# A planned order of work with new transfer and engine times, and a convolution whose taps are summed by TensorE for two blocks

## The chip, the cores and the metric

The kernel runs on one core of a Trainium2 chip. The metric is the device time of one execution in microseconds (us); lower is better. TensorE does the matrix products, VectorE (DVE) and ScalarE (ACT) the elementwise work, SyncE (SP) issues nearly all transfers.

## The reference

A softmax-weighted causal convolution over 7 tokens, then two MLPs with 2048 hidden units, on 8192 tokens of 192 features:

```python
def _attn_ref(x, weight_gen):                    # x (2, 4096, 192), weight_gen (2, 4096, 8, 7)
    w = softmax of weight_gen over its last axis
    x_unf = the 7 tokens up to each token, zeros in front
    out = np.einsum('bshk,bskhg->bshg', w, x_unf)
def _moe_ref(x, w_in, w_out):
    h = np.maximum(x @ w_in, 0.0)
    return h * h @ w_out
def _moe2_ref(x, w_in, w_out):
    h = x @ w_in
    return (h * np.clip(h + 3.0, 0.0, 6.0) / 6.0) @ w_out
```

The weights of the MLPs come as 64-bit floats; everything else is 32-bit. Matrix products are made in a rounded 32-bit format from a high and a low part of each operand, three products for one.

## The kernel before

**Tiling.** Each of 128 partitions holds 64 tokens in a row. They are taken in 16 blocks of 4 tokens per partition (512 columns, N). A block goes through the convolution, the first MLP (m=0) and the second (m=1). A *step* (m, b, f) is one block against 2 of the 16 tiles of the hidden units, so there are 2 x 16 x 8 = 256 steps. Step i issues part A (18 half-height products into the PSUM tile `h`) and, three steps later (LAG), part B (20 half-height products into the accumulators `accN` and `accR`), woven together in `emit_pair` (L299 is where each product is issued; the three last steps have only B, at L357). Between A and B the elementwise work stands: `relu` (L382, ACT), `square` (L386, ACT) or `gate` (L395, DVE), `high` (L402, either), `low` (L408, DVE).

**The convolution** of a block (`convolve`) is 7 products on DVE (L614) and 6 additions on DVE (L628). Then, for every block but block 0, `turn` (L276, DVE) and `to_dram` (L285, four transfers) turn the result through a DRAM tile `xs`, `from_dram` (L268, two transfers) brings it back with features on partitions, and `split_hi` (L224) and `split_lo` (L230) make its two parts. Block 0 is turned on TensorE instead: `twice` (L242), `turn_pe` (L250), `split_pe_hi` (L256), `split_pe_lo` (L261). The softmax of a chunk is seven small instructions (L575 to L595), the exponential on ACT (L583). `load_first` issues ten transfers for block 0; `load_rest` brings the other half of chunk 0.

**The weights** of one group (2 hidden tiles) come by four transfers (`load_weights`, L89 and L95) into a tile `st` with two buffers, and are made into high and low parts by six instructions on DVE (L117, L130, L139, L154, L161 twice) and four on ACT (L124, L127, L148, L151). There are 8 groups for each MLP; step f of a block needs group f/2.

**The order.** All instructions are written out by a planner in the kernel's own code. Every piece of work is an `Op` with a guessed duration per engine, what it depends on, and which buffers it takes. A loop simulates four engines (PE, ACT, DVE, SP), starts on each the ready piece with the earliest due time, and so fixes the order in which each engine's queue is filled. On the chip each queue is in order: an instruction that waits holds all behind it. A guessed duration therefore changes no work, only the order. A transfer has one guessed time for its issue (0.15 to 0.7 us for a whole group) and a fixed time to landing.

**The order of steps.** Blocks 0 and 1 of the first MLP are woven from step 4 (WEAVE): a0 a1 a2 a3, then a4 c0 a5 c1 and so on, so block 1 is needed at step 5 and block 2 at step 16. Six blocks of the first MLP (LEAD) run before the first of the second, which is woven with the next block; then blocks of the two alternate; six blocks of the second MLP are left at the end.

Of the kernel before, what the change touches and what calls it, by code (L numbers as in the profile page):

```python
# [8 lines left out]
F32 = mybir.dt.float32  # L9
# [9 lines left out]
def conv_moe_moe2_kernel(  # L19
# [10 lines left out]
    nc = tc.nc  # L30
# [18 lines left out]
    LEAD = 6  # L49
# [18 lines left out]
    ps_a = ctx.enter_context(tc.tile_pool(name="ps_a", bufs=4, space=bass.MemoryType.PSUM))  # L68
# [122 lines left out]
    def load_first():  # L191
        chunk_tiles(0)
        xt = xc[0]
        nc.sync.dma_start(out=wc[0][:, 0:TB, :], in_=w_v[:, 0:TB, :])
        nc.sync.dma_start(out=xt[:, PAD:PAD + TB, :], in_=x_v[:, 0:TB, :])
        for b in range(B):
            nc.gpsimd.memset(xt[b * PB:b * PB + 1, 0:PAD, :], 0.0)

        for h0, h1 in ((PAD // 2, PAD), (0, PAD // 2)):
            for b in range(B):  # L200
                p0 = b * PB
                for r0, r1 in ((0, (PB - 1) // 16 * 16), ((PB - 1) // 16 * 16, PB - 1)):
                    nc.sync.dma_start(
                        out=xt[p0 + 1 + r0:p0 + 1 + r1, h0:h1, :],
                        in_=x_v[p0 + r0:p0 + r1, TPP - PAD + h0:TPP - PAD + h1, :],
                    )
# [30 lines left out]
    def twice(j, engine):  # L237
        if j == 0:
            xraw[0, 0] = x_tile()
        d = xraw[0, 0][:, j].rearrange("p (t h r) -> p t h r", t=TB, h=2)  # L240
        src = attn[0][:, :, j * HP:(j + 1) * HP].unsqueeze(2).to_broadcast([P, TB, 2, HP])
        copy_on(engine)(d, src)  # L242

    def turn_pe(j):
        if j % 2 == 0:
            xps[j] = ps_h.tile([P, 2, N], F32, tag="h", name="xt")
        d = xraw[0, 0][:, j].rearrange("p (t c) -> p t c", t=TB)
        pv = xps[j // 2 * 2][:, j % 2].rearrange("d (q t r) -> d t q r", q=Q, t=TB)
        for t in range(TB):
            nc.tensor.transpose(pv[:, t], d[:, t], ident)  # L250

    def split_pe_hi(j, engine):
        if j == 0:
            xs_in[0, 0] = [split_tile(n) for n in "hl"]
        n = min(2, NK - j)
        copy_on(engine)(xs_in[0, 0][0][:, j:j + n], xps[j][:, 0:n])  # L256

    def split_pe_lo(j):
        n = min(2, NK - j)
        hi, lo = [v[:, j:j + n] for v in xs_in[0, 0]]  # L260
        nc.vector.tensor_tensor(out=lo, in0=xps[j][:, 0:n], in1=hi.bitcast(F32), op=ALU.subtract)  # L261
# [240 lines left out]

    class Op:
        def __init__(self, fn, times, deps, takes, uses, lands):
            self.fn, self.times, self.takes, self.lands = fn, times, takes, lands
# [5 lines left out]
    WEAVE = 4  # L511
# [4 lines left out]
    HOP, SLOT, T0 = 0.1, 0.2158, 20.0  # L516
    ops, users, taken = [], {}, {k: [] for k in BUFS}

    def add(times, fn, deps=(), takes=(), uses=(), lands=0.0):
        o = Op(fn, times, list(deps), list(takes), list(uses), lands)  # L520
        ops.append(o)
        for key in o.takes + list(uses):
            if o not in users.setdefault(key, []):
                users[key].append(o)
        return o

    def two(cols):
        return 0.165 + 1.03e-3 * cols

    def act_t(cols):  # L530
        return 0.19 + 0.83e-3 * cols

    def cp(cols):
        return {"ACT": act_t(cols), "DVE": 0.165 + 0.52e-3 * cols}
# [6 lines left out]
    first_load = add({"SP": 0.7}, load_first, takes=[("xc", 0), ("wc", 0)], lands=3.0)  # L541
    rest_load = None
    for m in range(2):
        for g in range(NG):
            k = (m, g)
            deps = [(last, -99.0)] if last else [(first_load, -99.0)]
            ld = last = add({"SP": 0.3}, lambda k=k: load_weights(*k), deps, [("st", k)], lands=4.0)
            if rest_load is None:
                last = rest_load = add(
                    {"SP": 0.15}, load_rest, [(ld, -99.0)], uses=[("xc", 0), ("wc", 0)], lands=3.0  # L550
                )
            q = add({"DVE": 0.61}, lambda k=k: w_q(*k), [ld], [("q", k)], [("st", k)])
            r = add({"ACT": 0.84}, lambda k=k: w_relu(*k), [q], uses=[("q", k)])
            t0 = add({"ACT": 1.14}, lambda k=k: w_t0(*k), [ld], [("t", k)], [("st", k)])
            t1 = add({"DVE": 0.68}, lambda k=k: w_t1(*k), [ld], [("t", k)], [("st", k)])
            hb = add({"DVE": 1.08}, lambda k=k: w_hb(*k), [r], [("hb", k)], [("st", k), ("q", k)])
            hi_w[k] = add(cp(CAN), lambda e, k=k: w_hi(*k, e), [hb], uses=[("hb", k)])
            hi_r[k] = add(cp(CR), lambda e, k=k: r_hi(*k, e), [hb], uses=[("hb", k)])
            sc = add({"DVE": 0.56}, lambda k=k: w_sc(*k), [hb], uses=[("q", k), ("hb", k)])
            both = [sc, t0, t1]  # L560
            lo_w[k] = add({"DVE": 0.82}, lambda k=k: w_low(*k), both, uses=[("q", k), ("t", k)])
            lo_r[k] = add({"DVE": 0.29}, lambda k=k: r_low(*k), both, uses=[("q", k), ("t", k)])

    chunk_load = {0: first_load}
    soft = {}

    def softmax(c, t0, t1, load):
# [31 lines left out]
        o = add({"DVE": two(cols)}, s1, [load], [st], keys)  # L599
# [37 lines left out]

    conv = {}
    for b in range(NB):
        c, t0 = divmod(b * TB, CT)  # L640
        if b == 0:
            s = softmax(0, 0, TB, first_load)
        elif b == 1:
            s = softmax(0, TB, CT, rest_load)
        elif t0 == 0:
            chunk_load[c] = add(
                {"SP": 0.15}, lambda c=c: load_chunk(c), [(conv[b - 1], -99.0)], [("xc", c), ("wc", c)], lands=6.5
            )
            s = softmax(c, 0, CT, chunk_load[c])
        conv[b] = convolve(b, [s] + ([(conv[b - 1], -99.0)] if b else []))  # L650
# [30 lines left out]
    def x_chain(m, b, source):  # L681
# [4 lines left out]
        o = prev = add({"SP": 0.15}, lambda: from_dram(m, b), deps, [key], uses, lands=6.0 if m else 5.0)  # L686
# [4 lines left out]

    dups = [
        add(cp(N), lambda e, j=j: twice(j, e), [conv[0]], [("x", (0, 0))], [("a", 0)]) for j in range(NK)
    ]
    for j in range(1, NK):
        dups[j].deps.append((dups[0], -99.0))
    turns_pe = []
    for j in range(NK):
        key = ("h", ("xt", j // 2 * 2))
        deps = [dups[j]] + turns_pe[-1:]  # L700
        turns_pe.append(add({"PE": 0.9}, lambda j=j: turn_pe(j), deps, [key], [("x", (0, 0))]))
    splits = [("sh", (0, 0)), ("sl", (0, 0))]
    hi_pe, lo_pe = [], []
    for j in range(0, NK, 2):
        key, cols = ("h", ("xt", j)), min(2, NK - j) * N
        t = {"ACT": act_t(cols), "DVE": two(cols)}
        deps = [turns_pe[min(j + 1, NK - 1)]] + hi_pe[-1:]
        hi_pe.append(add(t, lambda e, j=j: split_pe_hi(j, e), deps, splits if j == 0 else [], [key] + splits))
        lo_pe.append(add({"DVE": two(cols)}, lambda j=j: split_pe_lo(j), hi_pe[-1:], uses=[key] + splits))
    x_ready = {(0, 0): lo_pe}  # L710
    prev = hi_pe[0]

    ready_g, step_ops = {}, []
    stored, fixed = {}, {}

    def prepare_x(m, b):
        if m == 0:
            t = add({"DVE": two(TB * D)}, lambda: turn(b), [conv[b]], [("pr", ("aT", b))], [("a", b)])
            w = add({"SP": 0.3}, lambda: to_dram(b), [t], [("xs", b)], [("pr", ("aT", b))], lands=2.0)
# [8 lines left out]
    def finish(m, b, step):  # L728
# [6 lines left out]
        if m == 0:  # L735
            stored[b] = add({"SP": 0.15}, lambda: store_y(b), [z[0], z[1]], [("ys", b)], zk, lands=2.7)
            due(stored[b], fixed[step] + 30)
            return
        s0 = add({"SP": 0.1}, lambda: store_z0(b), [z[0]], [("zs", b)], zk[:1], lands=2.0)
        f0 = add({"ACT": act_t(N)}, lambda: fold(b), [z[1], (s0, -99.0)], [("zq", ("u", b))], zk[1:])  # L740
        f1 = add({"DVE": two(N)}, lambda: fold_add(b), [f0], uses=[("zq", ("u", b))] + zk[1:])
        s1 = add({"SP": 0.1}, lambda: store_z1(b), [f1], uses=[("zs", b)] + zk[1:], lands=2.3)
        l1 = add({"SP": 0.3}, lambda: load_z(b), [s0, s1], [("zq", b)], [("zs", b)], lands=2.3)
        tz = add({"DVE": two(TB * D)}, lambda: turn_z(b), [l1], [("q", ("o", b))], [("zq", b)])
        so = add({"SP": 0.1}, lambda: store_out(b), [tz], uses=[("q", ("o", b))], lands=2.5)
        due(so, fixed[step] + 45)

    prev_pe = turns_pe[-1]
    for i in range(NS + LAG):
        A = steps[i] if i < NS else None  # L750
        Bs = steps[i - LAG] if i >= LAG else None
        deps, takes, uses = [(prev_pe, -HOP)], [], []
# [55 lines left out]
    def released(o):  # L808
        t = 0.0
        for d, lag in o.deps:  # L810
            same = len(o.times) == 1 and len(d.times) == 1 and o.times.keys() == d.times.keys()
            t = max(t, d.start + 1e-6, d.end + lag + (0.0 if same else HOP))
# [7 lines left out]
    def available(o, t):  # L820
        wait = t
        for cls, key in o.takes:
# [3 lines left out]
            if len(held) >= BUFS[cls]:  # L826
                for u in users[cls, held[-BUFS[cls]]]:
                    if u.end is None:
                        return float("inf")
                    wait = max(wait, u.end + HOP)  # L830
        return wait

    t = 0.0
    while len(order) < len(ops):
        later = float("inf")
        for e in ("PE", "ACT", "DVE", "SP"):
# [18 lines left out]
            best.end = free[e] + best.lands  # L855
            later = min(later, free[e])
# [53 lines left out]
```

## Time and profile before

| | |
|---|---|
| median of three runs | 1142.57 us (1141.55 to 1144.91) |
| the profiled execution | 1142.03 us, span 1140.2 us |
| first product of step 0 | 36.27 us after the span's start |
| last product | ends near 1134.3 us |

The span runs from the first to the last instruction; 1.83 us of the profiled execution lie outside it. PE is TensorE's products, PEld its weight loads, SPq the issue of transfers. TensorE was recorded at its high clock level for most of the span, and at a lower mean between 36 and 76 us.

### The profile page before, as it was taken

How to read it: one execution, taken by the hardware profiler on the slowest of the kernel's cores; microseconds unless marked ns; L12 is line 12 of the kernel's file. 1: busy time of each engine (PE TensorE's matmuls, PEld its weight loads, DVE VectorE, ACT ScalarE, POOL GpSimd, SP SyncE). 2: the span in 40 equal slices, each digit the busy share in tenths (PEclk: the TensorE clock that was granted, in tenths of full speed). 3: DMA queues.
4: the chain of work that ended last, by engine and by line, in shares of the span. 5: the costliest groups of instructions: out<-in, count | busy, mean ns of one | idle time of the engine just before them, and what ended most of it. 6: DMA issues, size and time to landing. Idle time of an engine off the chain costs nothing.

```text
span 1140.2 us, 23704 instructions
## 1 busy us (share of the span) xinstructions
PE 1072.3 (94%) x9722; PEld 930.5 (82%) x9722; DVE 937.5 (82%) x1011; ACT 601.9 (53%) x657; POOL 4.3 (0%) x11
## 2 busy tenths in 40 slices
PE   0579999999999999999999999999999999999998
PEld 0368878887888888788888888888888888888887
DVE  6969989899899898889888887675867768888886
ACT  2669888897565647656364544435253442233322
POOL 0000000000000000000000000000000000000000
PEclk9979999999999999999999999999999999999999
DMA  5442424542241423314132221202222221232101
GB/s 139 119 118 71 146 74 143 128 107 66 71 108 36 138 70 115 82 43 123 33 84 57 75 66 52 70 21 69 57 71 56 51 66 39 60 79 74 34 25 47
DMA packets 68756, 87.90 MB, mean 77 GB/s; under 512 B 5612, under 2 KB 44396, under 8 KB 67752
## 3 DMA queue, kind: packets, MB, share of 16 engines
q1 hardware_dynamic: 68504, 86.19, 27.9%
q8 instruction: 76, 1.25, 0.5%
q14 instruction: 32, 0.26, 0.1%
q10 hardware_dynamic: 144, 0.20, 0.0%
HBM read 59.89 MB, written 26.48 MB: 76 GB/s over the span
## 4 chain that ended last, share of the span: by engine, by line
PE 72%; DVE 12%; DMA 9%; ACT 2%; issue 2%; SPq 2%; DVEq 0%; ACTq 0%
PE h L299 34%; PE accN L299 22%; PE accR L299 15%; DMA x<-ys 4%; DVE gl L408 3%; DMA st<-in_moe_w_out_dram 2%; DVE pr L614 2%; DVE a L628 2%; DVE sl L230 1%; DVE g L395 1%; ACT g L382 1%; DMA x<-xs 1%; DMA xs<-aT 1%; ACT gh L402 1%; DMA zs<-z 1%
## 5 line engine op out<-in xcount | busy, mean ns | idle before, releaser
L299 PE MATMUL h<-sh,w 64*128 64x512 f32 x3072 | 618.9, 382 | 27.8 <-ACT w L148 15.3
L299 PE MATMUL accN<-gh,w 64*128 64x512 f32 x2024 | 519.9, 377 | 0.0
L382 ACT ACTIVATE g<-h 128x1024 f32<-128x1024 f32 x256 | 261.9, 1023 | 465.3 <-PE h L299 442.2
L299 PEld LDWEIGHTS h<-sh,w 64*128 64x128 f32 x3072 | 387.9, 189 | 78.3 <-ACT w L148 17.6
L299 PE MATMUL h<-sl,w 64*128 64x512 f32 x1536 | 442.7, 380 | 1.3 <-DVE sl L230 1.3
L299 PEld LDWEIGHTS accN<-gh,w 64*128 64x128 f32 x2024 | 378.3, 187 | 26.6
L408 DVE TENSOR_TENSOR gl<-g,gh 128x1024 fp32r<-128x1024 f32 x256 | 312.6, 1221 | 30.0 <-ACT gh L402 20.1
L299 PE MATMUL accR<-gl,r 64*128 64x512 f32 x1012 | 301.4, 378 | 3.7 <-DVE gl L408 3.5
L299 PE MATMUL accN<-gl,w 64*128 64x512 f32 x1012 | 301.4, 378 | 0.0
L299 PE MATMUL accR<-gh,r 64*128 64x512 f32 x1012 | 300.6, 377 | 0.0
L299 PEld LDWEIGHTS h<-sl,w 64*128 64x128 f32 x1536 | 240.6, 189 | 21.8 <-DVE sl L230 1.6
L299 PEld LDWEIGHTS accR<-gl,r 64*128 64x128 f32 x1012 | 188.6, 187 | 19.4 <-DVE gl L408 6.3
L299 PEld LDWEIGHTS accR<-gh,r 64*128 64x128 f32 x1012 | 189.1, 187 | 13.4
L299 PEld LDWEIGHTS accN<-gl,w 64*128 64x128 f32 x1012 | 188.6, 187 | 13.2
L402 DVE CAST gh<-g 128x1024 fp32r<-128x1024 f32 x136 | 94.1, 692 | 89.3 <-PE accN L299 87.8
L395 DVE SCALAR_TENSOR_TENSOR g<-g,h 128x1024 f32<-128x1024 f32 x128 | 155.5, 1215 | 8.4 <-ACT g L382 7.8
L402 ACT CAST gh<-g 128x1024 fp32r<-128x1024 f32 x120 | 125.1, 1042 | 22.5 <-PE accN L299 19.3
L386 ACT ACTIVATE g<-g 128x1024 f32<-128x1024 f32 x128 | 135.5, 1059 | 1.9
L628 DVE TENSOR_TENSOR a<-a,pr 128x768 f32<-128x768 f32 x96 | 91.6, 954 | 0.4
L614 DVE TENSOR_TENSOR pr<-xc,wc 128x768 f32<-128x768 f32 x96 | 90.8, 953 | 1.2 <-DMA xs<-aT 0.8
L230 DVE TENSOR_TENSOR sl<-x,sh 128x1536 fp32r<-128x1536 f32 x31 | 54.3, 1753 | 12.8 <-ACT sh L224 12.8
L250 PE MATMUL xt<-ident,x 128*128 128x128 f32 x12 | 2.8, 424 | 30.6 <-ACT x L242 30.6
(60 smaller groups left out, 328.0 us busy)
## 6 DMA issues: line engine op xcount, KB each, us to landing
x<-ys SPq DMA_DIRECT2D x32, 512.0 KB, 6.4
x<-xs SPq DMA_DIRECT2D x30, 384.0 KB, 4.9
xc<-in_x_dram SPq DMA_DIRECT2D x7, 1344.0 KB, 5.9
ys<-z SPq DMA_DIRECT2D x32, 256.0 KB, 2.3
st<-in_moe_w_in_dram SPq DMA_DIRECT2D x32, 192.0 KB, 3.6
xs<-aT SPq DMA_DIRECT2D x60, 96.0 KB, 3.4
zq<-zs SPq DMA_DIRECT2D x60, 96.0 KB, 2.3
out_dram<-o SPq DMA_DIRECT2D x15, 384.0 KB, 2.3
```

What stands on the lines that cost most here:

```text
L230: nc.vector.tensor_tensor(out=lo, in0=src, in1=hi.bitcast(F32), op=ALU.subtract)
L250: nc.tensor.transpose(pv[:, t], d[:, t], ident)
L299: return lambda: nc.tensor.matmul(ps, w[r], turns(x[r]), start=start, stop=stop)
L382: nc.scalar.activation(g, ps, AF.Relu, bias=3.0 if m else 0.0)
L386: nc.scalar.activation(g, g, AF.Square)
L395: nc.vector.scalar_tensor_tensor(out=g, in0=g, scalar=6.0, in1=h_ps[m, b, f], op0=ALU.min, op1=ALU.mult)
L402: copy_on(engine)(gh, g)
L408: nc.vector.tensor_tensor(out=gl, in0=g, in1=gh.bitcast(F32), op=ALU.subtract)
L614: nc.vector.tensor_tensor(out=dst, in0=xs, in1=ws.to_broadcast([P, TB, H, G]), op=ALU.mult)
L628: nc.vector.tensor_tensor(out=total(), in0=total(), in1=prods.pop((b, k)), op=ALU.add)
```

## The change

1. Blocks 0 and 1 (ON_PE = 2): the 7 products stay on DVE, each in a tile of its own; their sum is made by TensorE with two 32-bit products per tap against the identity (384 columns each) in an accumulator tile. Both blocks are turned on TensorE; block 1 leaves the path through DRAM. `twice` now reads PSUM, in two halves.
2. `load_first` is split into three pieces, so that the softmax of block 0 depends on the weights' transfer alone, and each tap on the transfer that it reads. The softmax of the second half of chunk 0 may be placed only after the last sum of block 0 has been placed.
3. The planner's guesses: every transfer has an issue time and a service time on one shared line, plus FLIGHT 1.6; a waiting compute piece counts it as LATE 1.0 later; PSUM or buffers read by TensorE come free SLACK 0.5 later; instruction times are lowered by some 0.1 us.
4. WEAVE 4 to 3: block 1 is needed at step 4. LEAD 6 to 8: eight blocks of the first MLP in front, eight of the second at the end.
5. The two accumulators of a block become one tile of two PSUM banks (2 buffers in place of 4).

```diff
-    LEAD = 6
+    LEAD = 8
-    def twice(j, engine):
+    def twice(b, j, engine):
...
+        src = attn[b][:, :, 0:2 * D].rearrange("p a (t d) -> p a t d", t=2)[:, :, :, j * HP:(j + 1) * HP]
+        for a in range(2):
+            copy_on(engine)(d[:, 2 * a:2 * a + 2], src[:, a].unsqueeze(2).to_broadcast([P, 2, 2, HP]))
...
+    FLIGHT = 1.6
+    LATE = 1.0
+    SLACK = 0.5
+    WEAVE = 3
+    ON_PE = 2
...
-            ld = last = add({"SP": 0.3}, lambda k=k: load_weights(*k), deps, [("st", k)], lands=4.0)
+            ld = last = add(
+                None, lambda k=k: load_weights(*k), deps, [("st", k)],
+                dmas=[(0.62, 1.1), (0.62, 0.9), (0.6, 0.72), (0.47, 0.38)],
+            )
...
+    def convolve_pe(b, deps):
...
+        def total(k):
+            if k == K - 1:
+                attn[b] = ps_a.tile([P, 2, N], F32, tag="acc", name="acc")
+            v = prods.pop((b, k)).rearrange("p t h g -> p (t h g)")
+            for a in range(2):
+                nc.tensor.matmul(
+                    attn[b][:, a, 0:2 * D], ident, v[:, a * 2 * D:(a + 1) * 2 * D], start=k == K - 1, stop=k == 0
+                )
...
+            t = add(
+                {"PE": 1.4}, lambda k=k: total(k), [o] + ([t] if t else []), [acc] if k == K - 1 else [], [key, acc]
+            )
...
-            s = softmax(0, 0, TB, first_load)
+            s = softmax(0, 0, TB, [w_first])
         elif b == 1:
-            s = softmax(0, TB, CT, rest_load)
+            s = softmax(0, TB, CT, [rest_load, (conv[0], -99.0)])
...
-        o = prev = add({"SP": 0.15}, lambda: from_dram(m, b), deps, [key], uses, lands=6.0 if m else 5.0)
+        o = prev = add(
+            None, lambda: from_dram(m, b), deps, [key], uses, dmas=[(0.6, 2.7 if m else 2.0), (0.6, 2.4 if m else 1.7)]
+        )
...
+            late = LATE if d.dmas and lag > -9 and not o.dmas else 0.0
+            t = max(t, d.start + 1e-6, d.end + lag + late + (0.02 if same else HOP))
```

## Rows read from the trace of the kernel before

**Rows 1.** The page, first part: busy us, share of the span, instructions.
```profile
span 1140.2 us, 23704 instructions
...
PE 1072.3 (94%) x9722; PEld 930.5 (82%) x9722; DVE 937.5 (82%) x1011; ACT 601.9 (53%) x657; POOL 4.3 (0%) x11
```

**Rows 2.** Busy time by stretch: stretch, length, each engine's busy us, granted clock, DMA.
```profile
36.20:80.00 43.80, 28.22 (x156) 21.14 (x158) 33.06 (x48) 24.51 (x31) 0.00 (x0) 0.81 0.58 154
...
124.50:200.00 75.50, 73.17 (x672) 63.80 (x674) 69.08 (x76) 63.34 (x72) 0.00 (x0) 1.00 0.41 120
200.00:280.00 80.00, 76.49 (x700) 65.50 (x698) 71.23 (x84) 67.52 (x79) 0.00 (x0) 1.00 0.42 103
...
500.00:960.00 460.00, 459.49 (x4252) 402.65 (x4250) 353.77 (x363) 208.22 (x217) 0.00 (x0) 1.00 0.24 63
...
1134.30:1140.20 5.90, 1.38 (x12) 1.22 (x12) 0.56 (x1) 1.07 (x2) 0.00 (x0) 0.76 0.19 67
```

**Rows 3.** Chain that ended last, in order of time: start, us, what.
```profile
81.63 1.08 PE h L299 x10
...
85.73 1.08 PE h L299 x10
```

**Rows 4.** Busy time by stretch, products of L299 alone (PE, PEld, clock, DMA).
```profile
36.20:124.50 88.30, 71.34 (x550) 58.02 (x550) 0.90 0.43 114
```

**Rows 5.** Timeline of the first 37 us: start, us, engine, line; idle before and releaser.
```profile
2.91 0.39 DVE L575 TENSOR_REDUCE st<-wc 128x32 f32<-128x224 f32 x1 [2.91 <-DMA wc<-in_weight_gen_dram]
...
3.76 0.39 ACT L583 ACTIVATE wc<-wc 128x224 f32<-128x224 f32 x1 [1.52 <-DVE wc L578]
...
11.33 1.05 ACT L127 COPY t<-st 128x768 uint16<-128x768 uint16 x1 [7.18 <-DMA st<-in_moe_w_out_dram]
11.76 0.39 DVE L575 TENSOR_REDUCE st<-wc 128x32 f32<-128x224 f32 x1 [8.04 <-DMA wc<-in_weight_gen_dram]
...
12.49 0.38 DVE L586 TENSOR_REDUCE st<-wc 128x32 f32<-128x224 f32 x1
...
13.94 0.96 DVE L614 TENSOR_TENSOR a<-xc,wc 128x768 f32<-128x768 f32 x1
14.81 0.95 DVE L614 TENSOR_TENSOR pr<-xc,wc 128x768 f32<-128x768 f32 x1
...
27.84 1.95 DVE L628 TENSOR_TENSOR a<-a,pr 128x768 f32<-128x768 f32 x2
...
30.59 2.79 PE L250 MATMUL xt<-ident,x 128*128 128x128 f32 x12 [30.59 <-ACT x L242]
...
36.27 0.80 PE L299 MATMUL h<-sh,w 64*128 64x512 f32 x2 [2.89 <-DVE sl L261]
```

**Rows 6.** Groups by line and shape of the first 122 us: busy, mean ns.
```profile
L130 DVE TENSOR_SCALAR t<-st 128x768 uint16<-128x768 uint16 x9 | 5.9, 658 | 0.0
```

**Rows 7.** Busy time by stretch, instructions that touch tile q alone (DVE, ACT).
```profile
0.00:124.50 124.50, 26.55 (x41) 6.70 (x8) 0.93 0.42 113
```

**Rows 8.** One line's instructions: count, ns min/median/max, first and last start.
```profile
L494 PE MATMUL ot<-x x8: 222/275/294, 1135.1 to 1136.1; 128*128 128x64 f32 x8
```

**Rows 9.** Timeline of 49 to 71 us.
```profile
49.28 0.98 DVE L276 STREAM_TRANSPOSE aT<-a 128x768 f32<-128x768 f32 x1
...
56.83 0.80 PE L299 MATMUL h<-sh,w 64*128 64x512 f32 x2 [5.06 <-ACT w L148]
...
65.28 1.47 ACT L224 CAST sh<-x 128x1536 fp32r<-128x1536 f32 x1 [7.36 <-DMA x<-xs]
...
70.62 0.79 PE L299 MATMUL h<-sh,w 64*128 64x512 f32 x2 [6.81 <-ACT w L148]
```

**Rows 10.** Busy time of PE in one stretch (busy, products, granted clock, DMA).
```profile
70.60:75.80 5.20, 5.18 (x24) 0.50 0.57 151
```

**Rows 11.** Timeline of two later places where PE waits.
```profile
148.91 1.47 ACT L224 CAST sh<-x 128x1536 fp32r<-128x1536 f32 x1 [4.46 <-DMA x<-xs]
...
151.36 0.48 PE L299 MATMUL h<-sh,w 64*128 64x512 f32 x2 [2.15 <-ACT g L382]
...
258.64 0.67 DVE L117 TENSOR_SCALAR q<-st 128x768 uint32<-128x768 uint32 x1 [3.68 <-DMA st<-in_moe_w_out_dram]
...
264.55 0.48 PE L299 MATMUL accR<-gl,r 64*128 64x512 f32 x1 [2.26 <-DVE gl L408]
```

More of the change, by code (lines that the diff above doesn't have):

```diff
@@ L316, in make_B @@
         if f == 0:
-            accs[m, b] = [ps_a.tile([P, N], F32, tag="acc", name=f"acc{n}") for n in "NR"]
+            acc = ps_a.tile([P, 2, N], F32, tag="acc", name="acc")
+            accs[m, b] = [acc[:, o] for o in range(2)]
         high, low = [[], []], [[], []]
@@ L540, in conv_moe_moe2_kernel @@
     last = None
-    first_load = add({"SP": 0.7}, load_first, takes=[("xc", 0), ("wc", 0)], lands=3.0)
+    both = [("xc", 0), ("wc", 0)]
+    w_first = add(None, load_w0, takes=both, dmas=[(0.42, 0.3)])
+    x_first = add(None, load_x0, [(w_first, -99.0)], uses=both[:1], dmas=[(0.43, 1.66)])
+    halos = []
+    for h in ((PAD // 2, PAD), (0, PAD // 2)):
+        dep = halos[-1] if halos else x_first
+        halos.append(add(None, lambda h=h: load_halo(*h), [(dep, -99.0)], uses=both[:1], dmas=[(0.42, 0.25)] * 4))
+    first_load = halos[-1]
     rest_load = None
@@ L551, in conv_moe_moe2_kernel @@
                 )
[L552 to L556, printed above, removed]
+            q = add({"DVE": 0.55}, lambda k=k: w_q(*k), [ld], [("q", k)], [("st", k)])
@@ L597, in s7 @@
             )
-        o = add({"DVE": two(cols)}, s1, [load], [st], keys)
+        o = add({"DVE": two(cols)}, s1, load, [st], keys)
         o = add({"DVE": two(cols)}, s2, [o], uses=[st] + keys)
@@ L636, in convolve, with needs, term @@
         return add(cost, lambda: summed(0), [o], uses=[("a", b), ("pr", (b, 0))])
+    def needs(b, k):
+        if b:
+            return []
+        return [x_first] if k == PAD else [halos[k < PAD // 2]]
+    def convolve_pe(b, deps):
+        c, t0 = divmod(b * TB, CT)
+        keys, acc = [("xc", c), ("wc", c)], ("acc", ("conv", b))
+        def term(k):
+            xs = xc[c][:, t0 + k:t0 + k + TB, :].rearrange("p t (h g) -> p t h g", h=H)
+            ws = wc[c].rearrange("p t (h k) -> p t h k", k=K)[:, t0:t0 + TB, :, k:k + 1]
+            prods[b, k] = att.tile([P, TB, H, G], F32, tag="pr", name="pr", bufs=2)
+            nc.vector.tensor_tensor(out=prods[b, k], in0=xs, in1=ws.to_broadcast([P, TB, H, G]), op=ALU.mult)
+        def total(k):
[6 more added lines that the diff above has]
+                )
+        o = t = None
+        for k in range(K - 1, -1, -1):
+            key = ("pr", (b, k))
+            more = ([o] if o else deps) + needs(b, k)
+            o = add({"DVE": two(TB * D)}, lambda k=k: term(k), more, [key], keys)
+            t = add(
+                {"PE": 1.4}, lambda k=k: total(k), [o] + ([t] if t else []), [acc] if k == K - 1 else [], [key, acc]
+            )
+        return t
     conv = {}
@@ L702, in conv_moe_moe2_kernel @@
[L702 to L710, printed above, removed]
@@ L711, in conv_moe_moe2_kernel, with x_on_pe @@
-    prev = hi_pe[0]
+    x_ready, x_turned = {}, {}
+    def x_on_pe(b):
+        nonlocal prev
+        deps = [conv[b]] + ([(prev, -99.0)] if prev else [])
+        acc = ("acc", ("conv", b))
+        dups = []
+        for j in range(NK):
+            t = {"ACT": 2 * act_t(N // 2), "DVE": 2 * (0.09 + 1.045e-3 * N // 2)}
+            dups.append(
+                add(t, lambda e, j=j: twice(b, j, e), deps + [(d, -99.0) for d in dups[:1]], [("x", (0, b))], [acc])
+            )
+        turns_pe, hi_pe, lo_pe = [], [], []
+        for j in range(NK):
+            key = ("h", ("xt", b, j // 2 * 2))
+            t = {"PE": 1.0}
+            turns_pe.append(add(t, lambda j=j: turn_pe(b, j), [dups[j]] + turns_pe[-1:], [key], [("x", (0, b))]))
+        splits = [("sh", (0, b)), ("sl", (0, b))]
+        for j in range(0, NK, 2):
+            key, cols = ("h", ("xt", b, j)), min(2, NK - j) * N
+            t = {"ACT": act_t(cols), "DVE": two(cols)}
+            deps = [turns_pe[min(j + 1, NK - 1)]] + hi_pe[-1:]
+            takes = splits if j == 0 else []
+            hi_pe.append(add(t, lambda e, j=j: split_pe_hi(b, j, e), deps, takes, [key] + splits))
+            t = {"DVE": two(cols)}
+            lo_pe.append(add(t, lambda j=j: split_pe_lo(b, j), hi_pe[-1:], uses=[key] + splits))
+        x_ready[0, b] = lo_pe
+        prev = hi_pe[0]
+        return turns_pe[-1]
@@ L713, in conv_moe_moe2_kernel @@
+    first_turn = x_on_pe(0)
     ready_g, step_ops = {}, []
@@ L829, in available @@
                         return float("inf")
-                    wait = max(wait, u.end + HOP)
+                    wait = max(wait, u.end + (SLACK if "PE" in u.times else HOP))
         return wait
-    t = 0.0
+    t = line_free = 0.0
     while len(order) < len(ops):
@@ L855, in conv_moe_moe2_kernel @@
             best.end = free[e] + best.lands
+            if best.dmas:
+                at = t
+                for issue, serve in best.dmas:
+                    at += issue
+                    line_free = max(line_free, at + FLIGHT) + serve
+                best.end = line_free
             later = min(later, free[e])
```

126 lines of the change are left out of this document (63 added, 63 removed).

## The prediction

> **What bounds the kernel now.** I read the page first: TensorE is busy for 94% of the span, DVE for 82% [rows 1], so TensorE's own work is the floor and the question is where it falls behind. The chain that ended last gives its rate: a full step of 38 half products takes 4.10 us [rows 3], 0.1079 us for each. The code issues 256 steps x 38 = 9728 of them, 1049.6 us. The span is 1140.2 us, so some 90 us are something else, and the table by stretch says where. I cut the span at four points: step 0 begins at 36.27 us [rows 5]; up to 124.5 us 550 half products ran [rows 4], which is about the 548 that stand before step 16 (16 x 18 + 13 x 20), where block 2 is first needed; the last product ends near 1134.3 us, and 5.9 us follow [rows 2].
>
> - Before step 0: 36.2 us.
> - Step 0 to 16: 88.3 us for 59.3 us of work (550 x 0.1079), so **29.0 us lost** [rows 3, 4].
> - After that: 1009.8 us for 9178 x 0.1079 = 990.3 us, so **19.5 us lost**.
> - End: 5.9 us. Sum 1140.2.
>
> The three losses have causes that the timeline names. **Before step 0**, DVE reduces the first weights at 2.91 us and is then idle for 8.04 us until 11.76, since the reduction for the second half of the chunk was placed ahead of the second reduction of the first half and its transfer had not landed; the exponential that block 0 needed ended at 4.15 us (3.76 + 0.39) [rows 5]. **Step 0 to 16**: block 1 was turned on DVE at 49.28 us, but ACT's copy of it started at 65.28, after 7.36 us of idling for the transfer from `xs`. Weight work stood behind it in ACT's queue, and TensorE waited 5.06 and 6.81 us for ACT's weights [rows 9]. After such a wait TensorE runs at its low level, 1.2 GHz: in 5.20 us it did 24 products at a granted clock of 0.50 [rows 10]; at 0.1079 us they are 2.6 us. **After step 16** the places are small and of one kind: ACT idles 4.46 us for block 3's transfer and TensorE then 2.15 us; DVE idles 3.68 us for weights and TensorE then waits 2.26 us [rows 11]. From 500 to 960 us PE is busy 459.49 of 460.00 us [rows 2]; nothing is to be had there.
>
> **The change part by part.**
>
> *Step 0 comes earlier.* The second half's softmax can no longer stand ahead of block 0's. After the exponential's end at 4.15, the second reduction may start near 4.2; in the trace 1.45 us lie from it (12.49) to the first tap product (13.94), so the first product starts near 5.65. Seven products at 0.87 us (13.94 to 14.81) are 6.1 us [rows 5]. One group of weights must be ready too: five of its six DVE instructions write or read tile q, 26.55 us for 8 groups, 3.3 us each, and L130 adds 0.66 [rows 6, 7], so 4.0 us. They can start when the weights land, 11.33 [rows 5], and I don't expect the added splits of the loads to move that. DVE's last product ends near 5.65 + 6.1 + 4.0 = 15.8, the last sum on TensorE near 17.2. From the last addition's end (27.84 + 1.95 = 29.8) to step 0 (36.27) there were 6.5 us of copying, turning and splitting [rows 5], which stay. Step 0 then starts at about 24, **12 us earlier**. Bounds: 20 if the weights come wholly between the products, 31 if TensorE's sums are slow (next).
>
> *TensorE gets new work.* Block 0's sums fall before step 0, where PE had nothing to do, and cost nothing as long as a tap isn't slower than DVE's 0.87 us plus what lies between. Block 1's sums and turns fall among steps 0 to 4, on the path. No row shows a 32-bit product of 384 columns. From below: a rounded 64x512 product costs 0.2158 us alone, or 0.16 for 384 columns, 0.32 a tap. From above: L494's 32-bit products of 64 columns have a median of 275 ns [rows 8], six of which are 1.65 us, 3.3 a tap. Nearest is L250, the same identity against 32-bit data: 12 of 128 columns in 2.79 us [rows 5], 0.233 each, so three are 0.70 for 384 columns and 1.40 for a tap of two products. I take 1.40. Block 1 adds 7 x 1.40 + 2.79 = **12.6 us** (bounds 5 to 26).
>
> Of TensorE the Trainium skill, "FP8 and Floating Point Precision", section "TensorE Precision Notes", says that true FP32 takes 4 passes through the array. By it a tap is an estimated 2 x 384 x 4 columns, 1.28 us at 2.4 GHz and 2.56 at 1.2; at the first the sum would come out 0.8 us lower, at the second it is the second rival below. No run here shows such a product yet.
>
> *The loss up to step 16.* What goes: block 1's round trip through DRAM with ACT's 7.36 us idle, and TensorE's waits of 5.06 and 6.81 us behind it; the low level after each of them (about 2.6 us each). DVE also loses 12 additions (two at 27.84 took 1.95 us [rows 5], so 11 us) and one turn of 0.98 [rows 9]. What comes: turning block 1 takes both buffers of `h`, so the step after it must wait until ACT and DVE have split it; that is a bubble of 3 to 5 us, since the same splits held step 0 for 2.89 us [rows 5]. Weaving from step 3 wants block 1 one step sooner, but weights one step later. Between step 0 and step 4 DVE has three groups of weights (12 us), a softmax and seven products (about 9 us), the low parts of block 1 and of two steps (some 5 us), 26 us, while TensorE has three A parts and one A and B (3 x 1.94 + 4.10 = 9.9 us) and the 12.6 added, 22.5 us. So some 4 us remain of that, 4 of the bubble, 4 of low level: **12 us in place of 29** (bounds 6 to 22).
>
> *The loss after step 16.* The new guesses put the real issue time and landing of a transfer into the plan, so work that waits for one is placed later in ACT's and DVE's queues; with LEAD 8 the second MLP's weights have 16 more steps (66 us) in which to be made. Both bear on the two waits of rows 11. I take **11 us in place of 19.5** (bounds 6 to 22: more of the first MLP alone is also more of the stretch in which DVE is busy 69.08 of 75.50 us [rows 2]). The blocks' total work is the same in either order, so LEAD itself adds none. Merging the accumulators changes no count of banks: nothing. End: same code, 5.9.
>
> **Sum**: 24.0 + 59.3 + 12.6 + 12 + 990.3 + 11 + 5.9 = 1115.1 us of span, 1116.9 with the 1.83 outside it. The profiled execution lies 0.5 below the median of the runs, so I forecast **1117**.
>
> **The rivals.**
> 1. *The later waits stay.* The plan is better on paper, but DVE at 91% is what is short, not the guesses. For it: after 124.5 us DVE and ACT are both nearly full [rows 2]. Against: the two longest waits begin with a transfer. Time: 1117 + 8.5 = 1125.
> 2. *TensorE sums at the low level.* Then a tap is 2.8 us: block 0's sums end at 6.6 + 19.6 = 26.2, step 0 starts at 32.7; block 1 costs 22.4; with 15 us lost, 32.7 + 59.3 + 22.4 + 15 + 990.3 + 11 + 5.9 = 1136.6, about 1139 as a run: no change. For it: TensorE comes from idleness, and after idleness rows 10 show the low level. Against: the level rises again under steady products; by 81.63 us steps are 4.10 us apart [rows 3]. The page named above gives this case its price.
> 3. *Nearly all hidden.* Step 0 at 21, 9 us added, 7 and 6 lost: 1101. For it: TensorE's waits before step 16 leave room for block 1's sums. Against: they are removed as well.
> 4. *Slower: the longer stretch of the first MLP alone.* Steps 16 to 63 are now all first MLP: each has two more ACT activations and the convolution on DVE. If ACT's and DVE's queues then hold TensorE in every step, 48 steps pay. It decides from 0.60 us a step (29 us, what separates 1117 from 0.3% slower); at 0.8 the time is 1155. Against: the same kind of stretch lost 2.3 us in 75.50 (PE busy 73.17) and 3.5 in 80.00 [rows 2], 0.13 to 0.18 a step.
> 5. *It doesn't do what it says*: DVE still stands still before block 0 is done, because another waiting instruction takes the place of the first. Step 0 stays near 32, and the time is 1125.
>
> **How the numbers follow.** Forecast 0.47; rival 1, 0.20; 2, 0.10; 3, 0.13; 4, 0.07; 5, 0.03. A measurement of this kernel tells some 0.3%, 3.4 us, from no change. Forecast, rivals 1, 3 and 5 are faster, and half of rival 2: 0.88; the other half of it is no change, 0.05; rival 4 slower, 0.07. The range reaches from 1100 to 1138: it leaves out rival 4, most of rival 2's upper half and the lower end of rival 3.
>
> **What would show it.** DVE without an idle time above 3 us between 3 and 12 us; step 0's first product between 21 and 28; no `xs` transfer of block 1; sums at about 1.3 to 1.4 us a tap once TensorE is at its high level; block 2's products starting near 108 us; fewer waits of DVE and ACT on transfers after that. I am wrong if step 0 starts after 31, if taps stay above 2.5 us, or if the stretch up to the second MLP loses more than 0.3 us a step.

## The result, and the profile after

The changed kernel takes **1107.29 us** (1105.94 to 1109.66) against 1142.06 us for the one before on the same chip: a ratio of 0.9695, 95% interval 0.9668 to 0.9721. The gain is 35 us; 25 were forecast, and the time lies inside the range. The profiled execution took 1109.66 us, the slowest of the four, with a span of 1107.9 us.

The page of the kernel after (busy us, share, instructions), with the lines that answer to [rows 1], and the number of transfers of the path through DRAM:

```profile
span 1107.9 us, 23767 instructions
...
PE 1085.2 (98%) x9790; PEld 938.3 (85%) x9790; DVE 933.8 (84%) x1028; ACT 591.2 (53%) x638; POOL 3.2 (0%) x11
...
x<-xs SPq DMA_DIRECT2D x28, 384.0 KB, 5.1
...
xs<-aT SPq DMA_DIRECT2D x56, 96.0 KB, 2.8
```

TensorE is busy for 98% of the span where it was 94%, and the transfers of block 1 are gone (two loads and four stores fewer than 30 and 60). DVE has scarcely less to do (933.8 for 937.5 us), though the 12 additions that the prediction took off it are gone: the planner now gives it 160 of `high`'s copies where it gave 136. The same stretches as in [rows 2], cut at step 16 (columns: length, PE, PEld, DVE, ACT, POOL, granted clock, DMA share, GB/s):

```profile
36.20:109.14 72.94, 67.29 (x546) 54.33 (x544) 69.40 (x95) 61.42 (x75) 0.00 (x0) 0.95 0.42 115
109.14:200.00 90.86, 90.69 (x840) 79.05 (x838) 89.61 (x115) 82.72 (x94) 0.00 (x0) 1.00 0.46 133
200.00:280.00 80.00, 80.00 (x744) 70.24 (x742) 74.01 (x80) 55.46 (x58) 0.00 (x0) 1.00 0.29 77
...
1101.40:1107.90 6.50, 1.59 (x12) 1.29 (x12) 1.25 (x2) 1.07 (x2) 0.00 (x0) 0.92 0.17 61
```

From 109 us on TensorE doesn't wait: 90.69 of 90.86 us, 80.00 of 80.00, where [rows 2] had 73.17 of 75.50 and 76.49 of 80.00. DVE is *fuller* there than before (89.61 of 90.86), and nobody waits for it.

The start, timeline of the kernel after (start, us, engine, line; in brackets the idle time before and its releaser), to be read against [rows 5]:

```profile
4.16 0.39 DVE L608 TENSOR_REDUCE st<-wc 128x32 f32<-128x224 f32 x1 [0.45 <-ACT wc L605]
...
5.61 1.83 DVE L673 TENSOR_TENSOR pr<-xc,wc 128x768 f32<-128x768 f32 x2
...
9.66 0.96 DVE L673 TENSOR_TENSOR pr<-xc,wc 128x768 f32<-128x768 f32 x1 [2.22 <-PE acc L680]
...
17.77 0.56 DVE L117 TENSOR_SCALAR q<-st 128x768 uint32<-128x768 uint32 x1 [0.72 <-DMA st<-in_moe_w_out_dram]
18.24 0.95 DVE L673 TENSOR_TENSOR pr<-xc,wc 128x768 f32<-128x768 f32 x1
...
25.70 2.93 PE L680 MATMUL acc<-pr,ident 128*128 128x384 f32 x4 [2.34 <-DVE pr L673]
...
28.56 0.79 PE L301 MATMUL h<-sh,w 64*128 64x512 f32 x2
...
32.22 1.56 PE L680 MATMUL acc<-pr,ident 128*128 128x384 f32 x4
```

The second reduction starts at 4.16 us instead of 12.49, the first product at 5.61 instead of 13.94. Step 0 starts at 28.56 instead of 36.27. One tap (one of the seven products, added up by TensorE in two matrix products) is recorded as four TensorE records.

For every kernel below three numbers are read from its trace: the start of step 0, the start of the 549th half product (step 16), and what was lost after it, which is the span less the end (5.9 us before, 6.5 after), less step 16's start, less 9180 x 0.1079 = 990.5 us. The runs on the changed kernel are given its 6.5 us of end, e10 the 5.9. Cut in this way the kernel before has 36.3, 122.8 and 21.0. (The prediction cut it at 124.5, 1.7 us later, and counted 19.5 lost after that point.)

| kernel | median us | ratio to before, 95% interval | step 0 | step 16 | lost after it |
|---|---|---|---|---|---|
| before | 1142.06 | 1 | 36.3 | 122.8 | 21.0 |
| after | 1107.29 | 0.9695, 0.9668 to 0.9721 | 28.6 | 109.1 | 1.8 |
| e10 before, softmax's place | 1145.96 | 1.0012, 0.9998 to 1.0026 | 35.1 | 124.0 | 24.9 |
| e4 guesses and softmax's place | 1122.20 | 0.9800, 0.9770 to 0.9830 | 34.6 | 121.0 | 2.1 |
| e3 after, old transfer guesses | 1138.24 | 0.9946, 0.9929 to 0.9962 | 40.3 | 122.9 | 15.5 |
| e11 new issue times alone | 1111.85 | 0.9727, 0.9710 to 0.9745 | 27.9 | 106.4 | 6.6 |
| e12 new landings alone | 1117.80 | 0.9775, 0.9758 to 0.9791 | 31.2 | 109.7 | 9.1 |
| e7 LATE 0 | 1107.36 | 0.9698, 0.9678 to 0.9717 | 27.2 | 105.6 | 2.2 |
| e1 LEAD 6 | 1108.40 | 0.9681, 0.9655 to 0.9707 | 27.6 | 108.2 | 2.8 |
| e2 block 1 not on TensorE | 1115.67 | 0.9770, 0.9751 to 0.9789 | 26.8 | 114.2 | 1.9 |
| e5 softmax free | 1108.51 | 0.9703, 0.9689 to 0.9718 | 33.5 | 102.7 | 6.5 |
| e6 WEAVE 4 | 1114.02 | 0.9753, 0.9738 to 0.9768 | 27.3 | 109.6 | 5.7 |
| e8 TensorE busy from the start | 1107.36 | 0.9681, 0.9664 to 0.9698 | 28.5 | 107.1 | 1.8 |
| e9 and behind the turns | 1105.94 | 0.9670, 0.9655 to 0.9684 | 27.5 | 104.1 | 3.2 |

The kernel before, timed beside each of them, stood between 1142.1 and 1144.6 us, so ratios are compared, not medians.

### The profile page after: what moved, and what is told of

Read it like the earlier page. It is cut to its first block, busy times and chain, and to the rows that moved or that the text cites. A ratio compares the mean times of both kernels' runs of the same rounds, so it can differ in the third digit from the quotient of the medians.

```text
span 1107.9 us, 23767 instructions
## 1 busy us (share of the span) xinstructions
PE 1085.2 (98%) x9790; PEld 938.3 (85%) x9790; DVE 933.8 (84%) x1028; ACT 591.2 (53%) x638; POOL 3.2 (0%) x11
## 3 DMA queue, kind: packets, MB, share of 16 engines
q1 hardware_dynamic: 67256, 85.01, 27.9%
## 4 chain that ended last, share of the span: by engine, by line
PE 91%; DVE 4%; ACT 1%; issue 1%; DMA 1%; SPq 1%; DVEq 0%; ACTq 0%
PE acc L301 47%; PE h L301 43%; DMA st<-in_moe_w_out_dram 1%; DVE gl L411 1%; PE acc L680 1%; DVE a L650 1%; ACT g L385 1%; DVE pr L636 1%; DVE hb L139 0%; PE acc L360 0%; SPq L204 0%; SPq L89 0%; ACT gh L405 0%; SPq L95 0%; DVE w L161 0%
## 5 line engine op out<-in xcount | busy, mean ns | idle before, releaser
L301 PE MATMUL acc<-gh,w 64*128 64x512 f32 x2024 | 518.9, 377 | 0.0
L301 PEld LDWEIGHTS acc<-gh,w 64*128 64x128 f32 x2024 | 377.3, 186 | 26.8
L301 PE MATMUL acc<-gl,w 64*128 64x512 f32 x1012 | 300.0, 377 | 0.0
L301 PE MATMUL acc<-gh,r 64*128 64x512 f32 x1012 | 300.0, 377 | 0.0
L301 PE MATMUL acc<-gl,r 64*128 64x512 f32 x1012 | 300.0, 377 | 0.0
L301 PEld LDWEIGHTS h<-sl,w 64*128 64x128 f32 x1536 | 239.0, 187 | 21.4 <-DVE sl L231 1.0
L301 PEld LDWEIGHTS acc<-gl,r 64*128 64x128 f32 x1012 | 188.7, 186 | 13.5
L301 PEld LDWEIGHTS acc<-gh,r 64*128 64x128 f32 x1012 | 188.6, 186 | 13.5
L301 PEld LDWEIGHTS acc<-gl,w 64*128 64x128 f32 x1012 | 188.7, 186 | 13.4
L405 ACT CAST gh<-g 128x1024 fp32r<-128x1024 f32 x96 | 100.1, 1042 | 1.4 <-PE acc L360 1.3
L423 DVE TENSOR_SCALAR z<-acc 128x512 f32<-128x512 f32 x29 | 20.0, 689 | 22.2 <-PE h L301 22.1
```

Of the source, the lines that this page charges most:

```text
L301: return lambda: nc.tensor.matmul(ps, w[r], turns(x[r]), start=start, stop=stop)
L405: copy_on(engine)(gh, g)
L423: nc.vector.tensor_scalar(out=dst, in0=src, scalar1=scale, scalar2=None, op0=ALU.mult)
```

## The experiments

**Theory**: the guessed transfer times in the plan removed the losses after step 16 and the idle DVE at the start; TensorE's sums gained the rest, before step 16. **Rivals**: DVE had too much to do and TensorE's sums relieved it; LEAD gave the second MLP's weights their time; the new rule on the softmax's place did the start. A further rival was not tested alone: the planner's other new values (instruction times, SLACK, the merged accumulators) are in every run below but e10.

**e10: the rule on the softmax alone, on the kernel before.**

```diff
-            s = softmax(0, TB, CT, rest_load)
+            s = softmax(0, TB, CT, [rest_load, (conv[0], -99.0)])
```

> The kernel before with one edit: the softmax of the second half of chunk 0 may be placed only behind block 0's convolution. By the prediction's first step this alone frees 7 to 8 us of DVE at the start: 1134 to 1138 us. Rival (its fifth: another waiting instruction takes the place of the first): the first weight instruction now stands ahead of block 0's second reduction and waits for its transfer until 11 us; no gain, 1139 to 1145 us.

The rival held: no gain (0.9998 to 1.0026). The timeline of e10 says why:

```profile
11.28 0.56 DVE L117 TENSOR_SCALAR q<-st 128x768 uint32<-128x768 uint32 x1 [7.61 <-DMA st<-in_moe_w_out_dram]
11.76 0.38 DVE L586 TENSOR_REDUCE st<-wc 128x32 f32<-128x224 f32 x1
```

The reduction stands at 11.76 us, as late as in [rows 5]; only what stands in front of it has changed. The planner, believing in weights that land early, puts the first weight instruction there.

**e4: the guesses without the sums.** From the changed kernel, all that TensorE takes over is put back, with LEAD and WEAVE; the new guesses, the three pieces of the first loads, the merged accumulators and the rule on the second half's softmax stay. One more thing goes back: block 0's softmax again waits in the plan for all the first loads and not for its weights alone.

```diff
-    LEAD = 8
+    LEAD = 6
-    WEAVE = 3
-    ON_PE = 2
+    WEAVE = 4
+    ON_PE = 1
...
-            s = softmax(0, 0, TB, [w_first])
+            s = softmax(0, 0, TB, [first_load])
...
-        conv[b] = (convolve_pe if b < ON_PE else convolve)(b, [s] + ([(conv[b - 1], -99.0)] if b else []))
+        conv[b] = convolve(b, [s] + ([(conv[b - 1], -99.0)] if b else []))
```

> The kernel before with the new guesses and the split of the first loads, and the second half's softmax placed behind block 0's convolution; all sums on DVE, block 1 through DRAM, LEAD 6, WEAVE 4. Theory (guesses account for the losses after step 16 and for the idle time at the start): step 0 near 28 to 31 us, less than 5 us lost after step 16, 1115 to 1122 us. Rival (what TensorE takes over is the greater part): 1128 to 1142 us.

The median is 0.2 us above the theory's interval, and step 0, at 34.6, comes later than it said: the second reduction does start early, at 4.10 us, but after one product DVE still waits for weights (timeline of e4):

```profile
10.86 0.56 DVE L117 TENSOR_SCALAR q<-st 128x768 uint32<-128x768 uint32 x1 [4.35 <-DMA st<-in_moe_w_out_dram]
```

The two halves are clear all the same: after step 16 only 2.1 us are lost, while step 16 itself starts at 121.0, hardly sooner than before. The stretches of e4, columns as above:

```profile
121.00:200.00 79.00, 79.00 (x734) 68.69 (x732) 77.10 (x98) 74.37 (x87) 0.00 (x0) 1.00 0.46 126
200.00:280.00 80.00, 80.00 (x742) 69.28 (x740) 77.23 (x87) 47.16 (x49) 0.00 (x0) 1.00 0.33 87
```

TensorE is busy for all of both, with DVE at 98 and 97% and the same six blocks in front. So the losses after step 16 were neither a lack of DVE's time nor of blocks in front; they were the order. In this plan a DVE that is full up holds nobody. Since e10 shows that the rule alone gives nothing, the 22 us of e4 belong to the planner's new guesses as a whole, with the split loads and the merged accumulators. The next run shows that among these the transfer guesses can't be left out.

**e3: the reverse**, the changed kernel with the old guesses for transfers alone.

```diff
-                dmas=[(0.62, 1.1), (0.62, 0.9), (0.6, 0.72), (0.47, 0.38)],
+                dmas=[(0.3, 4.0)],
...
-    LATE = 1.0
+    LATE = 0.0
...
-            if best.dmas:
...
-                best.end = line_free
```

> The changed kernel planned with the old guesses for transfers (one short issue time per group, a fixed time to landing, no shared line, LATE 0); durations of engines, the sums on TensorE, LEAD and WEAVE stay. Theory (the guesses for transfers removed the losses): DVE again stands early before something that has not landed, now the weights, whose first instruction is placed ahead of the end of block 0's softmax, so step 0 comes 4 to 7 us later; and 10 to 15 us of waits return after step 16; 1120 to 1130 us. Rival (DVE's relief by TensorE's sums did it): 1107 to 1113 us.

Most of the gain goes, more than was expected: 0.9946, 8 us above the theory's interval. Both of its signs are there, and both are larger. In the timeline of e3 DVE stands before weights that have not landed, twice, and step 0 comes at 40.3 us, 11.7 later than in the changed kernel:

```profile
11.01 0.56 DVE L117 TENSOR_SCALAR q<-st 128x768 uint32<-128x768 uint32 x1 [6.24 <-DMA st<-in_moe_w_out_dram]
...
15.90 0.56 DVE L117 TENSOR_SCALAR q<-st 128x768 uint32<-128x768 uint32 x1 [3.34 <-DMA st<-in_moe_w_out_dram]
```

and the waits after step 16 are back (a stretch of e3: PE 74.54 of 77.00):

```profile
123.00:200.00 77.00, 74.54 (x680) 63.75 (x678) 74.19 (x91) 68.40 (x80) 0.00 (x0) 1.00 0.36 104
```

15.5 us are lost after step 16, with the new instruction times, SLACK and merged accumulators all in place. So everything but the transfer guesses, TensorE's sums included, is worth 6 us together on the old transfer guesses. On the new ones, what e4 put back is worth 12 (0.9800 to 0.9695). A shorter chain helps little while something else stands in the queue.

**e11 and e12: which half of the guess.** e11 keeps the new issue times with the old times to landing, e12 late landings with the old issue times; neither has the shared line or LATE. In both, the plan counts a landing from the end of the issue.

```diff
+        if dmas:
+            o.lands = old[1]
```

> The changed kernel planned with the new issue times of transfers (SP is taken for 1.2 us by the two transfers of a block, 2.3 by a group of weights) and the old fixed times to landing, no shared line, LATE 0. Theory (the old plan's error was the issue time, which delays everything behind it in SP's queue): nearly all of the gain stays, under 4 us lost after step 16, 1105 to 1111 us. Rival (the landing was guessed too early): 1118 to 1135 us.

```diff
-            times = {"SP": sum(i for i, _ in dmas)}
+            times = {"SP": old[0]}
...
+        if dmas:
+            o.lands = sum(i + s for i, s in dmas) + FLIGHT - old[0]
```

> The reverse: SP is taken only for the old short issue times, but each transfer lands as late as the new guesses say, without the shared line, LATE 0. Theory (issue time is the error): SP's queue is planned too full, transfers leave later than planned, and 5 us or more are lost after step 16, 1112 to 1130 us. Rival (only the landing counts): 1105 to 1111 us.

e11 just missed its theory (1111.85 us; 6.6 lost where under 4 were expected). e12 came out as its theory said (1117.80 us; 9.1 lost), but the reason given, that the issue time is the error, doesn't follow. Each run brings back most of the gain (0.9727 and 0.9775 against 0.9946 with the old guesses), and e12 does so without the new issue times. Nor is e11 the issue time alone: since the landing is counted from a later end of issue, a group of weights lands in its plan 6.3 us after the issue begins (2.31 + 4.0), 7.0 in e12's (2.31 + 3.1 + 1.6) and 4.3 in the old one. So a later landing alone recovers most of it, and taking SP for the true issue time as well, at landings that are mostly no later, gains 6 us more. New issue times with unmoved landings were not run, and which of the two counts for more stays open. The 6.6 and 9.1 us lost after step 16 are gone in the changed kernel, which has both and the shared line; e7, next, shows that LATE isn't needed for it.

**e7: LATE 0.**

```diff
-    LATE = 1.0
+    LATE = 0.0
```

> The changed kernel with LATE 0 in place of 1.0: a piece that waits for a transfer is planned for the moment of the guessed landing. Theory (issue and service times carry most of it, the margin little): 2 to 5 us come back after step 16, 1109 to 1113 us. Rival (the margin is what keeps waiting work from blocking the queues): 1115 to 1125 us.

Both expectations missed: the margin changes nothing (0.9698).

**e1: LEAD 6.**

```diff
-    LEAD = 8
+    LEAD = 6
```

> The changed kernel with six blocks of the first MLP in front in place of eight. Theory (the new guesses and DVE's earlier start removed the 18 us that used to be lost after step 16): little comes back, 1107 to 1111 us, and TensorE stays busy for over 99% from 120 us on. Rival (the two more blocks gave the weights of the second MLP the time they need): the waits near 200 to 280 us return, 1113 to 1120 us.

The theory held: 0.9681, and 2.8 us lost after step 16. The two more blocks in front bring nothing that can be measured.

**e2: block 1 on DVE and through DRAM.**

```diff
-    ON_PE = 2
+    ON_PE = 1
```

> The changed kernel with only block 0 summed by TensorE; block 1 has its additions on DVE and goes through DRAM again. Theory (block 1's trip costs ACT's and TensorE's waits, and more than the 9 us that its sums cost on TensorE): step 16 starts 5 to 12 us later, 1112 to 1120 us. Rival (the two cancel): 1105 to 1110 us.

As the theory said: step 16 comes 5.1 us later and the ratio is 0.0075 higher, some 5 to 9 us. TensorE waits mostly in one piece (timeline of e2):

```profile
60.57 0.80 PE L301 MATMUL h<-sh,w 64*128 64x512 f32 x2 [14.40 <-ACT sh L225]
```

TensorE again waits for ACT's copy of block 1, which in [rows 9] started at 65.28 us and here at 59.04. e2 has block 0's sums on TensorE and comes to step 16 6.8 us sooner than e4; but it differs from e4 in LEAD, WEAVE and the plan of the first loads as well, so that share isn't shown to be the sums alone.

**e5: the softmax free again, in the changed kernel.**

```diff
-            s = softmax(0, TB, CT, [rest_load, (conv[0], -99.0)])
+            s = softmax(0, TB, CT, [rest_load])
```

> The changed kernel without the rule that the second half's softmax comes behind block 0's last sum. Theory (with true landing times in the plan the rule no longer matters): no idle time of DVE above 3 us before 12 us, 1104 to 1111 us. Rival (the rule is what removed the 8 us): DVE stands still again, 1113 to 1117 us.

The theory held: with the new landing times the rule doesn't matter (0.9703). The way there is instructive: DVE does block 1's softmax and products first, step 0 comes 5 us *later* (33.5), step 16 6 us *sooner* (102.7), and 4.7 us more are lost after it. Step 0's start, on which the prediction dwelt, says little by itself.

**e6: WEAVE 4.**

```diff
-    WEAVE = 3
+    WEAVE = 4
```

> The changed kernel with blocks 0 and 1 woven from step 4 in place of 3: block 1 is needed one step later, the fifth group of weights one step sooner. Theory (near step 4 TensorE waits some 4 us for block 1's split parts, and weights are not late): that wait shrinks, 1103 to 1107 us. Rival (weights are what is short there): 1108 to 1113 us.

Both expectations missed: it is slower, 0.9753. TensorE's wait for block 1's split parts shrinks only from 4.26 to 3.26 us (step at 59.41), and now it waits for block 2's as well (timeline of e6):

```profile
109.55 0.48 PE L301 MATMUL h<-sh,w 64*128 64x512 f32 x2 [2.40 <-ACT sh L225]
...
112.62 0.79 PE L301 MATMUL h<-sl,w 64*128 64x512 f32 x2 [2.58 <-DVE sl L231]
```

Block 2's turned rows leave for DRAM at 96.44 us, in the changed kernel at 92.93. Why DVE comes to block 2 later with this weaving was not followed further.

**e8 and e9: TensorE kept from idling.** Products of the identity with itself, 14 ahead of everything (e8), and 8 and 18 more behind the turns of blocks 0 and 1 (e9).

```diff
+        warm = ps_h.tile([P, 2, N], F32, tag="h", name="warm")
+        for _ in range(WARM):
+            nc.tensor.matmul(warm[:, 0, 0:P], ident, ident, start=True, stop=True)
```

> The changed kernel with 14 products of the identity with itself (128 columns, their result is read by nobody) at the very start, where TensorE idles until 6.7 us. Theory (the low level makes block 0's first taps 2.56 us long and holds DVE for 2.2 us): taps of 1.28 us from the start, DVE's wait at 9.7 us gone, step 0 one to two us earlier, 1103 to 1107 us. Rival (the weights' landing near 11 us and DVE's weight work set step 0): no change, 1106 to 1110 us.

```diff
             nc.tensor.transpose(pv[:, t], d[:, t], ident)
+        if j == NK - 1:
+            for _ in range(FILL[b]):
+                nc.tensor.matmul(xps[b, j][:, 1, 0:P], ident, ident, start=True, stop=True)
```

> As the one before, with 8 more such products behind the turn of block 0 and 18 behind that of block 1, in a bank that nobody reads, so that TensorE does not idle while DVE and ACT split. Theory (the low level after these two gaps costs about 1.3 us at block 1's first tap and 2.7 us from 57 to 62 us): 3 to 4 us less than the one before, 1100 to 1104 us. Rival (the fill is in the way of the step that waits, or the level falls all the same): 1104 to 1110 us.

For e8 the rival held. DVE's wait for TensorE's taps falls from 2.22 to 0.69 us, and DVE then waits for the weights instead (timeline of e8):

```profile
8.18 0.96 DVE L674 TENSOR_TENSOR pr<-xc,wc 128x768 f32<-128x768 f32 x1 [0.69 <-PE acc L681]
11.27 0.56 DVE L117 TENSOR_SCALAR q<-st 128x768 uint32<-128x768 uint32 x1 [2.13 <-DMA st<-in_moe_w_out_dram]
```

Step 0 starts at 28.5 as in the kernel after. In e9 the mechanism works: no low level is left behind block 1. One stretch of PE (busy, products, granted clock), first of the kernel after, then of e9:

```profile
57.20:62.50 5.30, 5.30 (x26) 0.51 0.81 209
```

```profile
57.20:62.50 5.30, 5.30 (x54) 1.00 0.53 144
```

Step 16 comes at 104.1, 5.0 us sooner than in the kernel after and 3.0 sooner than in e8; 1.4 more are lost behind it in either comparison. The time missed the theory: it is 1.4 us less than e8's where 3 to 4 were expected, inside the rival's interval though the level did not fall. The ratio, 0.9670 (0.9655 to 0.9684), overlaps those of e8 and of the kernel after, so that e9 beats them isn't shown.

## Why the prediction was right, and where it was off

The forecast was a sum; with the cut at step 16 it reads against the trace (spans; the forecast's own cut lay 1.7 us later in the kernel before):

| term | forecast | measured |
|---|---|---|
| start of step 0 | 24.0 | 28.6 |
| block 1's sums and turns, and losses, to step 16 | 12.6 + 12 | 21.4 (109.1 - 28.6 - 548 x 0.1079) |
| lost after step 16 | 11 | 1.8 |
| end | 5.9 | 6.5 |

The work itself, 59.1 us to step 16 and 990.5 behind it, is the same on both sides.

**The losses after step 16: the right mechanism, mis-sized, and this is what the forecast missed by.** It was put at 11 us, halfway, for fear that a DVE at 91% would hold TensorE whatever the plan; 1.8 lies below even its bound of 6. That the whole still came out within 10 us is partly luck, since the late step 0 makes up for half of this miss. e4 shows 2.1 us lost with DVE at 98%. A row with two causes in it, a full engine and instructions that wait for transfers [rows 2, 11], was read as if both had to go. The first rival is refuted by e4, and LEAD's share, which the forecast gave beside that of the guesses, by e1.

**Step 0's start was 4.6 us late.** The forecast named what frees DVE as the new place of the softmax; e10 and e5 show that the place frees nothing by itself and isn't needed. What lets the second reduction go early is the new guesses (4.10 us in e4, where the sums are on DVE). They aren't enough for step 0: in e4 DVE still waits 4.35 us for weights and step 0 comes at 34.6. What brings it from there to 28.6 is the sums, the plan of the first loads, or both; that wasn't separated. That the fifth rival exists was right (e10 is that case to the letter), but it was tied to the wrong part. The rest is sizes: block 0's first taps ran at half pace and held DVE for 2.22 us; the first instruction of the second group of weights was placed ahead of the last product and waited 0.72 us; and block 1's first tap stood ahead of step 0 in TensorE's queue, from 25.70 to 28.56 (in e9, where that tap runs at the high level, step 0 starts at 27.5). The bounds given, 20 to 31, hold it; the sign named, 21 to 28, just doesn't. e8 shows that the taps' pace isn't what sets step 0, since the weights' landing near 11 us takes over. e5 shows that this term is in truth no term: it moves against the next one.

**TensorE's price.** The forecast took 1.40 us for a tap. At the high level a tap takes TensorE 1.49 us in the row at 32.22 (the next product starts at 33.71), and two in a row 2.78, from 39.47 to 42.25; at the low level 2.86 (25.70 to 28.56), the 2.8 of the second rival. The estimate was right by luck: L250's 12 turns, from which it came, took 2.79 us in [rows 5] after 30 us of idleness; in the kernel after, with TensorE busy just before, block 0's take 2.09:

```profile
21.27 2.09 PE L252 MATMUL xt<-ident,x 128*128 128x128 f32 x12 [0.46 <-ACT x L244]
39.47 2.85 PE L680 MATMUL acc<-pr,ident 128*128 128x384 f32 x8
42.25 0.48 PE L301 MATMUL h<-sh,w 64*128 64x512 f32 x2
```

The price came from the low level, as it seems, where a tap costs twice as much: in the kernel before, the 18 half products that follow the turn run at half pace too, 4.13 us where 18 x 0.1079 is 1.94 (columns: length, PE, granted clock, DMA share, GB/s):

```profile
36.20:40.40 4.20, 4.13 (x18) 1.00 0.00 0
```

So turning and summing don't have the same price per column: 2.09 us for 12 x 128 columns, 1.39 for 2 x 384. The second rival didn't come about, since only three of the 14 taps ran at the low level, the first two of block 0 and the first of block 1. The rule of the Trainium skill, "FP8 and Floating Point Precision", section "TensorE Precision Notes" (four passes for true FP32), gave estimates of 1.28 and 2.56 us; the trace agrees, with 0.1 to 0.3 us on top. The weight loads of the taps, two to a product, start 0.64 us apart at the low level:

```profile
8.13 0.34 PEld L680 LDWEIGHTS acc<-pr,ident 128*128 128x128 f32 x1 [0.30 <-issue]
8.77 0.34 PEld L680 LDWEIGHTS acc<-pr,ident 128*128 128x128 f32 x1 [0.30 <-issue]
```

**The stretch to step 16** came within 3.2 us: 21.4 for 24.6. Block 1's sums and turn add 10.9 us where 12.6 were forecast, since one of its taps ran ahead of step 0 (six taps 8.6, the turn 2.29). Of the losses, the bubble of 3 to 5 us behind block 1's turn is there, 4.26 us, and the low level after it (26 products in 5.30 us, where 54 ran in e9) comes to the 4 us forecast: 2.5 there and 1.5 in step 0, whose 18 half products take 3.66 us (28.56 to 32.22) where the next step's take 2.14 (33.71 to 35.85). The third part, 4 us of waiting for a DVE that falls behind, is the one that didn't come: TensorE waits 1.25 us for DVE's copy ahead of the turn.

```profile
50.65 2.29 PE L252 MATMUL xt<-ident,x 128*128 128x128 f32 x12 [1.25 <-DVE x L244]
57.20 0.80 PE L301 MATMUL h<-sh,w 64*128 64x512 f32 x2 [4.26 <-DVE sl L263]
```

Block 1's trip was rightly seen as worth more than its sums cost (e2). But one row was misread on the way: of TensorE's two waits for ACT's weights [rows 9], the 5.06 us end at 56.83, before ACT began to wait for block 1's transfer, so only the 6.81 stand behind that trip.

**The slower rival** asked whether 48 steps of the first MLP alone would each lose 0.6 us. In the kernel after, this stretch loses nothing: 80.00 of 80.00 us.

Of the 35 us, the planner's guesses without the sums keep some 22 (e4), and what e4 put back adds 12 on top. On the old transfer guesses all the rest together gives only 6 (e3 against before). The 22 and the 6 can't be added up, because the new instruction times, SLACK, the split loads and the merged accumulators are in both runs.

## What to carry to other kernels

Where a program plans the order of its queues, its guesses of when transfers are issued and land are part of the kernel's speed: with the same arithmetic a better set of guesses gave 22 us here, going back to the old transfer guesses cost 29 on the changed kernel (e3), and an engine at 98% held nobody once the order was right. An instruction moved from the front of a blocked queue uncovers the next that was planned by the same wrong guess (e10), so mend the guess, not the instruction. And price an operation at the clock level at which the row ran: a row of another operation, as it seems at another level, agreed here only by accident.

## What the runs showed of the hardware

The granted clock reads 1.00 from the start of a span although TensorE runs at half pace: in the kernel after, the weight loads of the taps are 0.64 us apart between 6.7 and 11.3 us, then four take 1.16 us, and both stretches' rows have 1.00:

```profile
6.70:11.30 4.60, 4.58 (x8) 1.00 0.89 247
11.30:14.40 3.10, 3.06 (x10) 1.00 1.04 244
11.27 1.16 PEld L680 LDWEIGHTS acc<-pr,ident 128*128 128x128 f32 x4 [0.24 <-issue]
```

Eight records in 4.60 us and then ten in 3.10 (two on the border count in both) show the change that the clock column doesn't. The row of the kernel before at 36.20 us, further up, is another case: half pace with 1.00 in the column. [Rows 10], after a first change has been recorded, has 0.50 for half pace.
